# Eight buffers for W2's tiles, and one weight set loaded in one run

## The chip, the core and the metric

The kernel runs on one core of one Trainium2 chip. The core has a matrix engine (TensorE, PE in the profile; its weight loads are PEld), a vector engine (DVE), a scalar engine (ACT), GpSimd (POOL) and a sync engine (SP), each with its own stream of instructions, which wait for each other by semaphores. Sixteen DMA engines move data between the chip's main memory, SBUF and other places in SBUF; in this kernel transfers are issued by SP and by ACT, each in the order of its stream (SPq and ACTq in the profile). The metric is the device time of one execution in microseconds (us).

## What is computed

A transformer block with attention and a gated MLP side by side, on one sequence of 2048 tokens of width 576, in bfloat16:

```python
def _A_ref(x, wqkv, wo):
    B, S, D = x.shape
    H = 32; Dh = D // H; W = 256
    ...
    scores = jnp.einsum("bhqd,bhkd->bhqk", q, k) * (Dh ** -0.5)
    mask = (idx[:, None] - idx[None, :] >= 0) & (idx[:, None] - idx[None, :] < W)
    ...
    return (lambda x, *d: x.transpose(*d))(o, 0, 2, 1, 3).reshape(B, S, D) @ wo

def _B_ref(x, w1, w3, w2):
    gate = jnp.einsum("bsd,df->bsf", x, w1)
    up = jnp.einsum("bsd,df->bsf", x, w3)
    h = _silu(gate) * up
    out = jnp.einsum("bsf,fd->bsd", h, w2)
    return out

x = A_x
xn = _layernorm(x, axis=-1)
return x + _A_ref(xn, A_wqkv, A_wo) + _B_ref(xn, B_w1, B_w3, B_w2)
```

There are 32 heads of width 18, the attention looks back 256 tokens, and the MLP's inner width is 4608.

## The kernel before

The tokens are cut into four chunks of 512 (`NC` = 4, numbered 0 to 3). Every chunk goes through the same stages on TensorE:

- the q, k and v projections (`proj_part`, L437), whose results ACT and DVE put into `stage` and `va`; DMA copies (L502) move q and k from `stage` into the layout that the scores need (`qv`, `kv`), eight groups of four heads;
- 36 units (`unit_pairs`, L664): a unit makes 128 of the 4608 inner columns, gate and up, by nine pairs of matmuls of 64 rows, the two of a pair side by side. Five pairs read the normalized input from `xnT`, four from `xnS`, a copy with the two halves of the partitions exchanged (L402). ACT (L673) and DVE (L679, L682) make the unit's column of `hT` of it. Between the units stand the score matmuls (L557), eight groups in turn, with their exponentials on ACT (L566) and masks on POOL (L593), and the products with v (`pv`, L614);
- the W2 stage (`p2_list`, `p2_item`): two halves of 288 output columns, each with nine tiles of W2 (`fc` = 0 to 8), so 18 tiles a chunk. A tile is 512 x 288 numbers (288 KB) in an SBUF buffer of 128 x 4 x 288 and is read by 16 matmuls (L715). At a half's last tile, the attention's output is multiplied with `wo` into the same banks (L721, reading `oT`), DVE adds x (L728) and SP stores the result (L730). The last pair of head groups' `pv` stands after the 20th item of the W2 stage, and the six copies that bring its result into `oT` follow on SP (`o_pack`, L651).

**Gate/up weights.** A chunk needs nine weight sets of W1 and W3, each for four units. A set is loaded by six transfers of 192 KB on SP (`load_part`, L323). They rotate over three buffers, `w13_0` to `w13_2`; the fourth set of chunk 0 goes into columns 18 to 26 of `hT`, which are still empty then. `owed` counts transfers that are allowed; `owe_part` issues one after the fourth and one after the last pair of a unit, each waiting for the matmul named. The last set of each chunk lies in `w13_1`, and the next set for that buffer, the next chunk's third, is asked for during the next chunk's projections. So `w13_1` holds nothing of use during the W2 stage.

**W2's tiles.** There are four buffers, `w2_0` to `w2_3`. A running count over all chunks picks the buffer. The first four loads are issued by SP in units 20 to 26 of chunk 0. Each later one is issued on ACT when the last matmul of a tile is written down, so it waits for that tile's matmuls and goes into its buffer: tile i's end asks for tile i + 4, and the last four tiles of a chunk ask for the first four of the next.

**The rows of x.** `load_x` (L299) loads 128 rows. Chunk 1's first two are asked for in the projections of chunk 0, after the key copies that `span_last(0, 2)` issues; the other two in units 8 and 17. Their first use is the layer norm's statistics (L358) from unit 20 on.

What orders DMA on an engine is the order in which the program writes the instructions: a transfer that waits for a semaphore holds up all that stand behind it on the same engine.

Of the kernel before, what the change touches and what calls it, by code (L numbers as in the profile page):

```python
# [164 lines left out]
def bass_parallel_sum__sliding_block__glu_gated_swiglu__prompt_kernel(  # L165
# [18 lines left out]
    NC = S // CH  # L184
# [13 lines left out]
    with ExitStack() as es:  # L198
# [96 lines left out]
        def load_x(t, eng="sp"):  # L295
            nonlocal xp_ctr
            s = xp_ctr % NXP
            xp_ctr += 1
            add(eng, lambda e: e.dma_start(xp[s][:], x2[t * 128:(t + 1) * 128, :]), w=[("xp", s)], dma=f"xp{s}")  # L299
            return s  # L300
# [37 lines left out]
                owed -= 1  # L338
                load_part((op,))

        n2fill = 0

        def load_w2(eng="sp"):
            nonlocal n2fill
            if n2fill >= NC * 2 * NFC:
                return
            s = n2fill % NW2
            half, fc = divmod(n2fill % (2 * NFC), NFC)
            n2fill += 1
            add(eng, lambda e: e.dma_start(  # L350
                w2[s][:], B_w2[fc * 512:(fc + 1) * 512, half * HD:(half + 1) * HD].rearrange("(fl p) d -> p fl d", p=128)),
                w=[("w2", s)], dma=f"w2_{s}")


        def ln_stats(t, s, part):
# [331 lines left out]
        def p2_list(c):  # L687

            seq = []
            for half in range(2):  # L690
                base = c * 2 * NFC + half * NFC
                for fc in range(NFC):
                    sl = (base + fc) % NW2
                    edge = fc == NFC - 1 or (half == 1 and fc == 0)
                    pairs = [(fl, tt) for fl in range(4) for tt in range(TB)]
                    if edge:
                        pairs = [(fl, tt) for tt in range(TB) for fl in range(4)]
                    for n, (fl, tt) in enumerate(pairs):
                        seq.append(("w2", half, fc, fl, tt, sl, n == len(pairs) - 1))
                        if fc == NFC - 1 and fl == 3:  # L700
                            seq += [("wo", half, fc, kd, tt, sl, False) for kd in range(5)]
                            seq.append(("out", half, fc, 0, tt, sl, False))
            return seq
# [3 lines left out]
        def p2_item(c, item, xs):  # L707
            nonlocal of_ctr
            what, half, fc, k, tt, sl, last = item
            d0 = half * HD  # L710
            bank = PS[:, ACC[tt], 0:HD]
            key = [("ps", ACC[tt])]
            if what == "w2":
                f = fc * 4 + k
                add("pe", lambda e: e.matmul(  # L715
                    bank, hT[:, f, tt * 128:(tt + 1) * 128], w2[sl][:, k, :], start=(f == 0), stop=False),
                    r=[("h", f), ("w2", sl)], **{"w" if f == 0 else "j": key})
                if last:
                    load_w2("act")
            elif what == "wo":  # L720
                add("pe", lambda e: e.matmul(  # L721
                    bank, oT[:, k, tt * 128:(tt + 1) * 128], wo[:, k, d0:d0 + HD], start=False, stop=(k == 4)),
                    r=[("oT", j) for j in range(G // 2)] + ["oTz", "wo", "woz"], j=key)
            else:
                o = of_ctr % NOF
                of_ctr += 1
                t = c * TB + tt
                add("dve", lambda e: e.tensor_tensor(ofin[:, o, :], bank, xp[xs[tt]][:, d0:d0 + HD], ALU.add),  # L728
                    r=key + [("xp", xs[tt])], w=[("of", o)])
                add("sp", lambda e: e.dma_start(out2[t * 128:(t + 1) * 128, d0:d0 + HD], ofin[:, o, :]),  # L730
                    r=[("of", o)], dma=f"out{o}")
# [93 lines left out]
        for what in [("q", 0), ("q", 1), ("q", 2), ("q", 3), ("8", 7), None]:  # L825
            got = proj_begin(0, what) if what else proj_end()
            if got == ("q", 0):
                load_w13((), 4)
                span_main(0, 2, "act")
                load_w13((), 2)  # L830
            elif got == ("q", 2):
                span_last(0, 2)
                for t in (TB, TB + 1):
                    xslot[t] = load_x(t)

        PV_COST, PV_AFTER = 6.6, 20
        main, rest = span_main, span_last
# [5 lines left out]
        for c in range(NC):  # L843
# [3 lines left out]
            plan = near if c + 1 < NC else {}  # L847
            stat, apply, xt = ({v[k]: i for i, v in plan.items()} for k in range(3))
            loads = {8: (2,), 17: (3,)} if c + 1 < NC else {}
            total = 9 * NF + len(att) + 3 * PV_COST  # L850
            if c:
                total += 9 * sum(COST[kind] for kind, _ in PROJ)
# [59 lines left out]
            for u in range(NF):  # L912
                at_u = u
                if c == 0 and u == 0:
                    owed += 12
                if u in loads:
                    for i in loads[u]:
                        xslot[(c + 1) * TB + i] = load_x((c + 1) * TB + i)
                b0 = jobs[u] = job()
                for n in range(9):  # L920
                    into = nxt - (clock + 9 - n)
                    if done < len(att) and (clock >= nxt or (n == 8 and into < 3 and clock >= soon)):
                        spaced_step()
                    op = unit_pairs(c, u, n, n + 1, b0[0])
                    clock += 1
                    if n in (3, 8):
                        owe_part(op)
                unit_tanh(u, b0[0])
                if u % 4 == 3 and u < NF - 4 and (c or u != 15):
                    owed += 6  # L930
                if next_pv in pv_ready and clock >= pv_ready[next_pv] and next_pv < 3:
                    j = next_pv
                    next_pv += 1
                    banks = job()
                    pv(c, j, banks)
                    clock += PV_COST
                    for g in (2 * j, 2 * j + 1):
                        for s in range(NS):
                            if pt_of[(c, g, s)][0] != "h":
                                free.append(pt_of[(c, g, s)])  # L940
                    later(u, lambda b=banks: (pv_out(b[0], 0), pv_out(b[1], 1), o_scale(0)))
                    later(u + 1, lambda j=j: (o_turn(2 * j, 0), o_turn(2 * j, 1), o_scale(1)))
                    later(u + 2, lambda j=j: o_turn(2 * j + 1, 0))
                    later(u + 3, lambda j=j: (o_turn(2 * j + 1, 1), o_pack(j, "sp")))
                unit_h(u, b0[0])
                for what in side.pop(u, []):
                    what()
                if u in stat:
                    t = (c + 1) * TB + stat[u]
                    for part in range(2):  # L950
                        ln_stats(t, xslot[t], part)
                if u in xt:
                    xn_send((c + 1) * TB + xt[u])
                if u in apply:
                    t = (c + 1) * TB + apply[u]
                    ln_apply(t, xslot[t])
                for span, a, b, n0, n1, eng in late_spans.get(u, []) if c == 0 else []:
                    span(a, b, only=slice(n0, n1), **({"q_eng": eng} if span is main else {"eng": eng}))
                if c == 0 and u in (8, 9, 10, 11):
                    buf, key = ((wo, "woz"), (oT, "oTz"))[(u - 8) // 2]  # L960
                    part = buf[64:128, 4, :] if u % 2 else buf[96:128, 0:4, :]
                    add("dve", lambda e, part=part: e.memset(part.bitcast(dt.float32), 0.0), **{"j" if u % 2 else "w": [key]})
                if c == 0 and u == 13:
                    for t in range(4):
                        rows = A_wo[252 * (t // 2):252 * (t // 2) + 252, :].rearrange("(s p d) f -> p s d f", p=2, d=Dh)[t % 2, :, :, :]
                        add("sp", lambda e, t=t, rows=rows: e.dma_start(wo[0:126, t, :], rows),
                            r=["woz"], dma="wo", **{"j" if t else "w": ["wo"]})
                    add("sp", lambda e: e.dma_start(wo[0:72, 4, :], A_wo[504:576, :]), r=["woz"], j=["wo"], dma="wo")
                if c == 0 and u in (20, 22, 24, 26):
                    load_w2()  # L970
                if u == 29:
                    xs = [load_x(c * TB + tt) for tt in range(TB)]
            assert done == len(att) and next_pv == 3, (done, next_pv)
# [4 lines left out]
            if c + 1 < NC:  # L978
                for g in range(G):
                    keep_keys(g)  # L980
            banks = ()
            for n, item in enumerate(p2_list(c)):
                p2_item(c, item, xs)
# [54 lines left out]
```

## Time and profile before

| | us |
|---|---|
| median of 3 runs | 562.51 |
| lowest and highest of the 3 | 562.33, 562.85 |
| the profiled execution | 562.53 |
| its span in the profile | 560.8 |
| TensorE busy | 555.4 |
| DVE, ACT, POOL busy | 314.8, 253.1, 163.1 |

The granted TensorE clock was 1.00 in the profiled execution. By its matmul starts, the stages lie as follows: chunk 0's units begin at 21.98 us, and the W2 stages of chunks 0 to 3 begin at 102.12, 239.90, 377.90 and 516.29. The page of the profile holds, for the whole execution, the busy time of each engine, a row of digits for 40 equal slices (9 means 90% or more), the chain of work that ended last, and groups of instructions by line. The views of the trace show instructions in order of time (start, duration, engine, line, operation, tile, and in brackets the idle time before it with what ended it), the chain in order of time, and the busy time of each engine within chosen windows. In such windows the last three numbers are the granted clock, the DMA share, and GB/s. Every DMA adds to its semaphore as its parts land; "landing" is the last of these increments, which the trace holds with its time.

### The profile page before, as it was taken

The page shows a single profiled execution, that of the slowest core. Times are in us where ns is not written, and L with a number is a line of the kernel's source. Part 1 is how long each engine was busy: PE and PEld are TensorE (multiplying, and loading weights), DVE is VectorE, ACT ScalarE, POOL GpSimd, SP SyncE. Part 2 cuts the span into 40 slices and gives each one's busy share as a digit, 9 for nine tenths or more (in the row PEclk, how much of TensorE's full clock was granted, in tenths as well). Part 3 has the DMA queues.
Part 4 walks back from the last instruction along what each step waited for, and adds up shares of the span by engine and source line. Part 5 has one row for each costly group of instructions (what it writes and reads, how often), then busy time and mean ns, then how long its engine had stood idle before and what let it go on. Part 6 is the DMA issues. An engine that isn't in the chain of part 4 may idle for free.

```text
span 560.8 us, 15711 instructions
## 1 busy us (share of the span) xinstructions
PE 555.4 (99%) x6767; PEld 343.9 (61%) x6767; DVE 314.8 (56%) x587; ACT 253.1 (45%) x349; POOL 163.1 (29%) x383
## 2 busy tenths in 40 slices
PE   8999999999999999999999999999999999999998
PEld 4445455677665455477766645547777654555776
DVE  7468788710465778851046668883114567767211
ACT  4357776100287776600037776650004676675000
POOL 6313454400034445330003344532000333433000
PEclk9999999999999999999999999999999999999999
DMA  9988879886366467587626754868752675460552
GB/s 249 206 192 179 198 171 203 196 215 176 87 143 145 117 146 165 139 200 206 170 67 139 169 129 111 161 177 189 194 145 59 138 172 131 113 162 12 139 148 64
DMA packets 126685, 85.83 MB, mean 153 GB/s; under 512 B 34024, under 2 KB 124320, under 8 KB 126616
## 3 DMA queue, kind: packets, MB, share of 16 engines
q1 hardware_dynamic: 89076, 63.16, 49.5%
q10 hardware_dynamic: 37540, 21.66, 14.7%
q8 instruction: 53, 0.87, 0.7%
q14 instruction: 16, 0.13, 0.1%
HBM read 71.29 MB, written 2.36 MB: 131 GB/s over the span
## 4 chain that ended last, share of the span: by engine, by line
PE 97%; DMA 2%; DVE 1%; issue 0%; POOL 0%
PE ps L664 50%; PE ps L715 24%; PE ps L437 9%; PE ps L557 6%; PE ps L614 4%; PE ps L721 3%; DMA w<-in_B_w_dram 1%; DMA xp<-in_A_x_dram 0%; DVE xn L370 0%; DVE stats L358 0%; DVE stats L360 0%; DVE mv L361 0%; POOL rstd L364 0%; PE ps L382 0%; DVE ofin L728 0%
## 5 line engine op out<-in xcount | busy, mean ns | idle before, releaser
L664 PE MATMUL ps<-xnT,w 64*128 64x512 bf16 x1400 | 181.3, 376 | 0.1
L664 PE MATMUL ps<-xnS,w 64*128 64x512 bf16 x1120 | 153.9, 376 | 0.0
L715 PE MATMUL ps<-w,hT 128*128 128x288 bf16 x1152 | 147.3, 286 | 0.2 <-DMA w<-in_B_w_dram 0.2
L566 ACT ACTIVATE pt<-ps 128x1024 bf16<-128x1024 f32 (+1 forms) x112 | 113.1, 1010 | 63.4 <-PE ps L557 63.1
L679 DVE SCALAR_TENSOR_TENSOR gs<-th,ps 128x512 bf16<-128x512 bf16 x144 | 97.8, 679 | 77.8 <-ACT th L673 76.7
L715 PEld LDWEIGHTS ps<-w,hT 128*128 128x128 bf16 x1152 | 111.9, 98 | 30.9 <-issue 1.7
L664 PEld LDWEIGHTS ps<-xnT,w 64*128 64x128 bf16 x1400 | 69.9, 94 | 58.6 <-issue 0.5
L593 POOL TENSOR_TENSOR pt<-pt,mk 128x128 int32<-128x128 int32 (+1 forms) x199 | 80.3, 425 | 79.5 <-ACT pt L566 79.5
L682 DVE SCALAR_TENSOR_TENSOR hT<-gs,ps 128x512 bf16<-128x512 bf16 x144 | 98.9, 687 | 5.0
L673 ACT ACTIVATE th<-ps 128x512 bf16<-128x512 f32 x144 | 85.4, 593 | 24.0 <-PE ps L664 23.7
L664 PEld LDWEIGHTS ps<-xnS,w 64*128 64x128 bf16 x1120 | 57.0, 94 | 52.5
L728 DVE TENSOR_TENSOR ofin<-ps,xp 128x288 bf16<-128x288 f32 x32 | 14.6, 457 | 120.2 <-PE ps L721 120.2
L450 ACT ACTIVATE stage<-ps 128x512 bf16<-128x512 f32 x16 | 9.6, 597 | 146.1 <-PE ps L437 143.8
L593 POOL TENSOR_TENSOR hT<-hT,mk 128x128 int32<-128x128 int32 (+1 forms) x31 | 12.4, 421 | 170.7 <-ACT hT L566 170.7
L557 PE MATMUL ps<-qv,kv 64*128 64x320 bf16 (+4 forms) x528 | 52.5, 260 | 0.0
L557 PEld LDWEIGHTS ps<-qv,kv 64*128 64x128 bf16 x528 | 27.3, 94 | 25.8 <-issue 0.3
L437 PE MATMUL ps<-xnT,wp 64*128 64x512 bf16 (+1 forms) x360 | 38.7, 355 | 0.0
L566 ACT ACTIVATE stage<-ps 128x1024 bf16<-128x1024 f32 x24 | 24.6, 1023 | 12.6 <-PE ps L557 12.6
L636 DVE STREAM_TRANSPOSE od<-oq 128x256 bf16<-128x256 bf16 x64 | 25.8, 427 | 6.3 <-POOL oq L629 6.3
L437 PEld LDWEIGHTS ps<-xnT,wp 64*128 64x128 bf16 x360 | 19.0, 94 | 14.1 <-issue 0.7
L721 PE MATMUL ps<-wo,oT 128*128 128x288 bf16 x160 | 24.8, 286 | 0.0
L593 POOL TENSOR_TENSOR stage<-stage,mk 128x128 int32<-128x128 int32 (+1 forms) x42 | 17.0, 423 | 17.4 <-ACT stage L566 17.2
(59 smaller groups left out, 341.9 us busy)
## 6 DMA issues: line engine op xcount, KB each, us to landing
w<-in_B_w_dram SPq DMA_DIRECT2D x210, 192.0 KB, 4.1
w<-in_B_w_dram ACTq DMA_DIRECT2D x68, 288.0 KB, 3.1
xp<-in_A_x_dram SPq DMA_DIRECT2D x29, 144.0 KB, 4.3
out_dram<-ofin SPq DMA_DIRECT2D x32, 72.0 KB, 1.7
xnS<-xnT SPq DMA_DIRECT2D x8, 256.0 KB, 4.3
oT<-od SPq DMA_DIRECT2D x56, 36.0 KB
pt<-in_A_wqkv_dram SPq DMA_DIRECT2D x4, 288.0 KB, 6.5
hT<-in_B_w_dram SPq DMA_DIRECT2D x6, 192.0 KB, 5.1
```

What stands on the lines that cost most here:

```text
L437: op = add("pe", lambda e, out_=out_, st=st, mv=mv, n=n, r0=r0, first=first: e.matmul(out_, st, mv, start=first, stop=(part == 1 and n == ...
L557: add("pe", lambda e, r0=r0, out_=out_, kb=kb, q0=q0, nb=nb: e.matmul(out_, kb4[r0:r0 + 64, g, kb + NV - NB, :] if kb < 0 else kv[r0:r0 + ...
L566: add("act", lambda e: e.activation(pt_slot(sl)[:, 0:w, :], PS[:, SC[0]:SC[1] + 1, 0:w].rearrange("p r q -> p q r"), ACT.Exp, scale=scale) ...
L593: add("pool", lambda e, vb=vb, mm=mm: e.tensor_tensor(vb, vb, mm, ALU.mult), r=(key if n == 0 else []) + ["mk"], **{"w" if n == 0 else "j" ...
L614: add("pe", lambda e, p=p, q=q, pr=pr, sl=sl, g=g, pos=pos, q0=q0, nb=nb, col=col, first=first, n=n: e.matmul(PS[32 * q:32 * q + VW, banks ...
L636: add("dve", lambda e: e.transpose(od[i][:, g % 2, c0:c0 + CH // 2], oq[:, c0:c0 + CH // 2]), r=["oq", "oq0"], **{"j" if half or g % 2 els ...
L664: op = add("pe", lambda e, n=n, r0=r0, r=r, k=k, src=src: e.matmul(PS[:, b0 + r, :], wt[r0:r0 + 64, k, fl * 128:(fl + 1) * 128], src, star ...
L673: add("act", lambda e: e.activation(th[i][:], PS[:, bg, :], ACT.Tanh, scale=0.5), r=[("ps", bg)], w=[("th", i)])
L679: add("dve", lambda e: e.scalar_tensor_tensor(out=gs[i][:], in0=th[i][:], scalar=1.0, in1=PS[:, bg, :], op0=ALU.add, op1=ALU.mult), r=[("t ...
L682: add("dve", lambda e: e.scalar_tensor_tensor(out=hT[:, u, :], in0=gs[i][:], scalar=0.5, in1=PS[:, bu, :], op0=ALU.mult, op1=ALU.mult), r= ...
L715: add("pe", lambda e: e.matmul(bank, hT[:, f, tt * 128:(tt + 1) * 128], w2[sl][:, k, :], start=(f == 0), stop=False), r=[("h", f), ("w2", ...
L721: add("pe", lambda e: e.matmul(bank, oT[:, k, tt * 128:(tt + 1) * 128], wo[:, k, d0:d0 + HD], start=False, stop=(k == 4)), r=[("oT", j) fo ...
```

## The change

W2's tiles rotate over eight buffers in place of four. The four new ones are views of `w13_1` (`w2x`). `w2_at` picks the buffer: of each eight tiles of a chunk the first four go into `w2`, with a start that moves by two from chunk to chunk, the next four into `w2x`. At the start of each W2 stage, behind the last matmul of unit 35, ACT issues the loads of tiles 4 to 7 at once; then the end of tile i asks for tile i + 8 (i below 10), the ends of tiles 10 and 11 for the next chunk's tiles 0 and 1, and those of 16 and 17 for its tiles 2 and 3. Tiles 12 to 15 ask for nothing. SP still issues chunk 0's first four in units 20 to 26.

In chunk 0, the third weight set's six transfers are issued in one run after `span_last(0, 2)`, with no wait for matmuls, and `owed` starts with 6 instead of 12. The four x loads of chunk 1 move to units 11, 13, 15 and 17; in the other chunks they stay.

```diff
+        w2x = w13[1][:, :, :].rearrange("p a b -> p (a b)")[:, 0:NW2 * 4 * HD].rearrange("p (n k d) -> p n k d", n=NW2, d=HD)
+
+        def w2_at(c, i):
+            n = i % (2 * NW2)
+            if n < NW2:
+                s = (n + 2 * c) % NW2
+                return s, w2[s]
+            return n, w2x[:, n - NW2, :, :]
+
+        def load_w2(c, i, eng="act", after=()):
+            if c >= NC:
+                return
+            s, dst = w2_at(c, i)
+            half, fc = divmod(i, NFC)
             add(eng, lambda e: e.dma_start(
...
+                w=[("w2", s)], after=after, dma=f"w2_{s}")
+
+        def next_w2(c, i):
+            if i < 10:
+                load_w2(c, i + 8)
+            elif i < 12:
+                load_w2(c + 1, i - 10)
+            elif i >= 16:
+                load_w2(c + 1, i - 14)
...
-                base = c * 2 * NFC + half * NFC
                 for fc in range(NFC):
-                    sl = (base + fc) % NW2
+                    sl = half * NFC + fc
...
+                buf, wt = w2_at(c, sl)
                 add("pe", lambda e: e.matmul(
-                    bank, hT[:, f, tt * 128:(tt + 1) * 128], w2[sl][:, k, :], start=(f == 0), stop=False),
-                    r=[("h", f), ("w2", sl)], **{"w" if f == 0 else "j": key})
+                    bank, hT[:, f, tt * 128:(tt + 1) * 128], wt[:, k, :], start=(f == 0), stop=False),
+                    r=[("h", f), ("w2", buf)], **{"w" if f == 0 else "j": key})
                 if last:
-                    load_w2("act")
+                    next_w2(c, sl)
...
             elif got == ("q", 2):
                 span_last(0, 2)
-                for t in (TB, TB + 1):
-                    xslot[t] = load_x(t)
+                load_w13()
...
             loads = {8: (2,), 17: (3,)} if c + 1 < NC else {}
+            if c == 0:
+                loads = {11: (0,), 13: (1,), 15: (2,), 17: (3,)}
...
                 if c == 0 and u == 0:
-                    owed += 12
+                    owed += 6
...
                 if c == 0 and u in (20, 22, 24, 26):
-                    load_w2()
+                    load_w2(0, (u - 20) // 2, "sp")
...
+            for i in range(NW2, 2 * NW2):
+                load_w2(c, i, after=(last_pe(),))
```

More of the change, by code (lines that the diff above doesn't have):

```diff
@@ L339, in owe_part @@
                 load_part((op,))
[L341 to L345, printed above, removed]
+        w2x = w13[1][:, :, :].rearrange("p a b -> p (a b)")[:, 0:NW2 * 4 * HD].rearrange("p (n k d) -> p n k d", n=NW2, d=HD)
[7 more added lines that the diff above has]
+            if c >= NC:
                 return
-            s = n2fill % NW2
-            half, fc = divmod(n2fill % (2 * NFC), NFC)
-            n2fill += 1
+            s, dst = w2_at(c, i)
+            half, fc = divmod(i, NFC)
             add(eng, lambda e: e.dma_start(
-                w2[s][:], B_w2[fc * 512:(fc + 1) * 512, half * HD:(half + 1) * HD].rearrange("(fl p) d -> p fl d", p=128)),
-                w=[("w2", s)], dma=f"w2_{s}")
+                dst[:, :, :], B_w2[fc * 512:(fc + 1) * 512, half * HD:(half + 1) * HD].rearrange("(fl p) d -> p fl d", p=128)),
+                w=[("w2", s)], after=after, dma=f"w2_{s}")
[6 more added lines that the diff above has]
+                load_w2(c + 1, i - 14)
         def ln_stats(t, s, part):
```

## The prediction

> **What bounds the kernel now.** I read the page's shares first, then the chain of waits, then TensorE's timeline for gaps between matmul starts, then the windows for how full the DMA engines are.
>
> ```profile
> PE 555.4 (99%) x6767; PEld 343.9 (61%) x6767; DVE 314.8 (56%) x587; ACT 253.1 (45%) x349; POOL 163.1 (29%) x383
> DMA  9988879886366467587626754868752675460552
> PE 97%; DMA 2%; DVE 1%; issue 0%; POOL 0%
> L715 PE MATMUL ps<-w,hT 128*128 128x288 bf16 x1152 | 147.3, 286 | 0.2 <-DMA w<-in_B_w_dram 0.2
> w<-in_B_w_dram ACTq DMA_DIRECT2D x68, 288.0 KB, 3.1
> ```
>
> TensorE is busy 555.4 of 560.8 us and holds 97% of the chain, so only its gaps and its pace can be won. The pace is even: by the starts in the trace, the W2 matmuls (L715) follow each other every 122 or 123 ns, and the gate/up matmuls (L664), which start in pairs, every 215 to 217 ns a pair. Outside the first 10 us (warm-up and layer norm, untouched) three starts break it. One is in the gate/up loop:
>
> ```profile
> 35.58 1.24 PE L664 MATMUL ps<-xnT,w 64*128 64x512 bf16 x10
> 37.75 1.49 PE L664 MATMUL ps<-xnT,w 64*128 64x512 bf16 x10
> ```
>
> Ten matmuls that take 1.24 us take 1.49 here: a pair interval is 454 ns instead of 216, so 0.24 us. It is where unit 8 begins, the first reader of the third weight set. The set's last two parts are issued at 32.50 and 33.98 and take 4.1 us to land, so the last is there at 38.1; the reader was due at 37.97.
>
> The second is in chunk 2's W2 stage, and the chain shows it as time of a DMA:
>
> ```profile
> 399.57 1.97 PE ps L715 x16
> 401.56 6.05 DMA w<-in_B_w_dram
> 407.65 4.46 PE ps L715 x35
> ```
>
> A W2 tile asked for at 401.56, as its buffer came free, took 6.05 us beside the two 256 KB xnS copies of 400.5 and 401.1; with four buffers the cover was 5.9 us. The interval is 534 ns instead of 122: 0.41 us. A third, at 114.86, is 179 ns: 0.06 us. All three are waits for DMA, together 0.71 us of 560.8.
>
> **The change, part by part.** (1) Third weight set of chunk 0 in one run. Its six transfers no longer wait for matmuls of units 0 to 2 but stand in SP's queue where two x loads stood at 25.14. At 0.65 us an issue (3.00 us for 4 in the SP timeline, at most 0.75) they are out by 29.1 to 29.6 and, at the 4.1 to 5.2 us that these parts took to land, there by 34.8, 3 us ahead of 37.97. Gain 0.24 us, all on the path. Bounds: 0 if they were again late, 0.24 if not.
>
> What stands behind them moves too. The set in hT's columns follows at once (its waits are for units 0 to 2, over by 27.8), then three key copies of groups 2 to 4, formerly at 29.93, now at about 29.1 + 4 x 0.65 = 31.7. Even with the longest landing of that stretch (7.7 us) and two more issues, they are there by 41; the first score matmul of group 2 is the ninth score step, at 50.41. Nine us of cover, cost 0. The four x loads move to units 11, 13, 15, 17; their first reader is a statistic at 69.81, while unit 17 is at about 60: cost 0. The later sets of the chunk leave SP's queue earlier by up to two units, and are needed no earlier.
>
> (2) Eight W2 buffers. The count of loads (72 of 288 KB) and of matmuls is as before, and a matmul reading w13_1 instead of w2 has the same 128x288 form: 0. A tile is asked for eight tiles ahead, not four: cover grows from 5.9 to 13.7 us, against a slowest landing of some 6 us. Gain 0.41 + 0.06 = 0.47 us.
>
> (3) Four more loads at the start of each W2 stage, on ACT behind the last tanh.
>
> ```profile
> 102.23 0.60 ACT L673 ACTIVATE th<-ps 128x512 bf16<-128x512 f32 x1 [1.35 <-PE ps L664]
> 104.29 39.20 ACTq L350 DMA_DIRECT2D w<-in_B_w_dram  x18
> 146.80 0.60 ACT L450 ACTIVATE stage<-ps 128x512 bf16<-128x512 f32 x1 [43.97 <-PE ps L437]
> ```
>
> Four issues of 0.374 us fill 102.8 to 104.3, the gap before the load that tile 0's end releases at 104.29; ACT computes nothing until 146.80. ACT's cost is 0; without that gap, the next load would be at most 1.5 us later, with 13.7 us of cover. No later wait on ACT is added: the loads of tiles 12 to 15's turns are simply absent.
>
> But the transfers themselves come early, into a stretch where the DMA engines are full:
>
> ```profile
> 102.00:106.00 4.00, 4.00 (x97) 2.98 (x96) 3.41 (x7) 0.60 (x1) 3.51 (x10) 1.00 0.67 184
> 106.00:114.00 8.00, 8.00 (x67) 6.38 (x66) 2.93 (x8) 0.00 (x0) 1.35 (x2) 1.00 1.12 228
> 114.00:118.00 4.00, 4.00 (x35) 3.05 (x33) 0.00 (x0) 0.00 (x0) 0.00 (x0) 1.00 0.77 193
> 130.00:140.00 10.00, 10.00 (x84) 8.00 (x82) 0.00 (x0) 0.00 (x0) 0.00 (x0) 1.00 0.57 157
> 248.00:256.00 8.00, 8.00 (x67) 6.39 (x66) 0.56 (x2) 0.00 (x0) 0.00 (x0) 1.00 0.66 172
> 384.00:392.00 8.00, 8.00 (x68) 6.40 (x66) 1.68 (x5) 0.00 (x0) 0.72 (x2) 1.00 0.67 172
> ```
>
> The column before the last is the DMA share. In 130 to 140 only W2 tiles move, one per 1.96 us: 0.57 x 1.96 = 1.1 us of all sixteen engines for a tile (0.98 by 408 to 417, share 0.50). Four tiles are 3.9 to 4.5, say 4.2 us of extra work, at 102.6, at 240.4 and at 378.4. Who is late next? The last six oT copies (L651), due at the first wo matmul:
>
> ```profile
> 110.53 4.55 SPq L651 DMA_DIRECT2D oT<-od  x6
> 257.49 0.78 PE L721 MATMUL ps<-wo,oT 128*128 128x288 bf16 x5
> ```
>
> By the increments on their semaphore the last lands at 116.88, 255.03 and 393.00; wo starts at 119.47, 257.49 and 395.48: cover 2.6, 2.5 and 2.5 us. Does SP's small copy wait for ACT's backlog? In the first stage a small copy on ACT's otherwise empty queue (L502, issued 17.20) landed at 23.20, 6.0 us, while SP had eight large transfers under way; alone, at 147.43, the like took 2.0. So I count with service in order of issue, the dear case. Room that eats the backlog before the last oT copy: chunk 0, 0.33 x 4 + 0.23 x 1.3 = 1.6 us; chunk 1, full until 248 (share 1.00 from 238), then 0.34 x 6 = 2.0; chunk 2, 0.33 x 7.4 = 2.4. Left over as delay: 2.6, 2.2, 1.8 us. That just fits the cover; cost 0, the value I take. Bounds: 0, and 4.5 - 2.5 = 2.0 us a chunk, 6.0 in all, if no room were found. In chunk 3 no next chunk's weights load (share 0.40 over 516 to 561), cost 0.
>
> The Trainium skill, page "DMA: Bandwidth & Descriptors", section "Queues, rings and completion order", says that each DMA engine takes turns between the queues a packet at a time. By it the oT copies would hardly be delayed and the cost is 0 with room to spare; the row at 17.20 speaks against so clean a sharing.
>
> **Sum.** The profiled execution took 562.53 us (span 560.8 and 1.7 around it), 0.02 above the median, 562.51. 562.53 - 0.24 - 0.47 = 561.82, so 561.8 us, 0.13% less. Below 0.2% (1.1 us) a measurement of this kernel can't well be told from no change.
>
> **Rivals.** (A) The oT copies come late: the burst of four W2 tiles takes the DMA engines ahead of them, and TensorE stands at the first wo matmul of chunks 0, 1 and 2. It decides once the delay passes 2.5 us. For it: the share is above 1.00 in 106 to 114, my leftover for chunk 0 equals the cover, and 17.20 shows small copies waiting behind large ones. Against it: the shares leave room in chunks 1 and 2, and xnT, xnS and outputs have 5 us and more. Middle of the bounds, 0.9 us each: 561.8 + 2.7 = 564.5; to 567.8 at the end of the bounds; within 0.2% of before if only chunk 0 pays.
>
> (B) Nothing is won: the waits are so small (0.24, 0.41) that DMA jitter makes new ones, or the third set is late again since it now shares the engines with the q and k copies. 562.4. Against it: 3 us and 8 us of new cover.
>
> (C) The earlier weight transfers starve the attention of chunk 0: keys of group 2 after 50.41. It needs 9 us of delay; the longest landing there is 7.7. A missed score step would cost about 2 us: 563.8.
>
> (D) Faster by over 0.2%: that needs 1.1 us, and the trace shows 0.71 of waits; only waits that this one execution didn't have could give it. 561.2.
>
> **How the numbers follow.** Forecast 0.52; B 0.13; A 0.25 (0.20 of it above 0.2%, 0.05 within); C 0.02; D 0.08. Faster 0.08, same 0.52 + 0.13 + 0.05 = 0.70, slower 0.22. The likeliest case's own range is 561.4 to 562.4. For 8 in 10 the range goes to 561.2 below and into A up to 564.2, leaving half of D and the dearer half of A outside.
>
> **What would show it.** Right: unit 8's ten matmuls take 1.24 us; no L715 start interval above 135 ns but at the pv matmuls; the DMA piece is gone from the chain of chunk 2; ACT issues four loads at once after the last tanh; DMA share near 1.0 longer after 102, 240 and 378, and wo matmuls still starting about 17.35 us (chunk 0) after the W2 stage. Wrong: a gap before L721 in chunks 0 to 2, with oT landing more than 2.5 us after its old place (A); a new gap in units 8 to 16 (B, C).

## The result, and the profile after

| | us |
|---|---|
| before, median of 17 runs | 562.59 (562.10 to 563.22) |
| changed, median of 17 runs | 564.45 (563.15 to 565.89) |
| ratio | 1.0032, 95% interval 1.0023 to 1.0040 |
| the changed kernel's profiled execution | 565.61, span 563.8 |

The changed kernel is slower by 1.86 us, 0.3%. Its profiled execution is one of the dearer ones, 1.16 us above its median. The changed file is 13 lines longer above the places that matter, so L664, L715, L721 and L651 of before are L677, L728, L734 and L664 here, and the W2 loads of L350 are L355. On the page:

```profile
PE 555.4 (98%) x6767; PEld 350.1 (62%) x6767; DVE 314.9 (56%) x587; ACT 253.1 (45%) x349; POOL 163.5 (29%) x383
DMA  9998769993366457599335655869922674561730
L728 PE MATMUL ps<-w,hT 128*128 128x288 bf16 x1152 | 147.1, 286 | 0.0
L734 PE MATMUL ps<-wo,oT 128*128 128x288 bf16 x160 | 24.8, 286 | 3.2 <-DMA oT<-od 2.4
w<-in_B_w_dram ACTq DMA_DIRECT2D x68, 288.0 KB, 5.2
```

TensorE does the same 555.4 us of work in a span 3.0 us longer. The W2 matmuls (L728) no longer wait at all. The wo matmuls (L734), which never waited before, have 3.2 us of idle time ahead of them, put down to the DMA that fills `oT`. A W2 tile takes 5.2 us to land at the median; before, it took 3.1. The chain in order of time, in chunk 1's W2 stage:

```profile
253.77 6.45 DMA oT<-od
260.22 0.14 issue
260.36 0.77 PE ps L734 x5
```

and TensorE's timeline there:

```profile
255.75 2.74 PE L728 MATMUL ps<-w,hT 128*128 128x288 bf16 x21
260.36 0.77 PE L734 MATMUL ps<-wo,oT 128*128 128x288 bf16 x5 [1.87 <-DMA oT<-od]
```

The last of the six copies takes 6.45 us, and wo starts only when it is there. By matmul starts, the interval ahead of wo is 1.08 us in chunk 0, 2.16 in chunk 1 and 0.80 in chunk 2, against 0.12 where nothing waits: 0.95 + 2.03 + 0.67 = 3.65 us lost. The third weight set's gap is gone:

```profile
35.70 1.29 PE L677 MATMUL ps<-xnT,w 64*128 64x512 bf16 x10
37.86 1.29 PE L677 MATMUL ps<-xnT,w 64*128 64x512 bf16 x10
```

Unit 8's ten matmuls take as long as unit 7's. The 3.65 us lost and the 0.71 us of old gaps won give 2.94 us, and the two spans differ by 3.0. ACT's timeline at the start of chunk 0's W2 stage, and SP's when the copies are issued in chunk 1:

```profile
102.12 0.60 ACT L686 ACTIVATE th<-ps 128x512 bf16<-128x512 f32 x1 [1.35 <-PE ps L677]
102.13 42.13 ACTq L355 DMA_DIRECT2D w<-in_B_w_dram  x18
```

```profile
249.42 5.04 SPq L664 DMA_DIRECT2D oT<-od  x6
254.51 1.23 SPq L408 DMA_TRANSPOSE xnT<-xn  x1
```

The burst begins with the last tanh, and the six copies' issues take 5.04 us where they took 4.56 before. In the windows (the column before the last is the DMA share, the last GB/s):

```profile
102.00:106.00 4.00, 4.00 (x98) 3.04 (x97) 3.43 (x7) 0.60 (x1) 3.42 (x10) 1.00 0.95 232
106.00:114.00 8.00, 8.00 (x67) 6.38 (x66) 2.81 (x8) 0.00 (x0) 1.35 (x2) 1.00 1.19 222
114.00:118.00 4.00, 4.00 (x35) 3.20 (x33) 0.00 (x0) 0.00 (x0) 0.00 (x0) 1.00 1.14 261
130.00:140.00 10.00, 10.00 (x84) 7.98 (x83) 0.00 (x0) 0.00 (x0) 0.00 (x0) 1.00 0.23 61
248.00:256.00 8.00, 8.00 (x68) 6.37 (x67) 0.77 (x2) 0.00 (x0) 0.59 (x1) 1.00 1.16 262
```

The DMA share is now 0.95 to 1.19 from 102 to 118, it is 1.16 in 248 to 256, where it was 0.66, and 0.23 from 130 to 140, where it was 0.57: the work came forward. In 106 to 114 the share rose from 1.12 to 1.19, but the rate did not, 222 GB/s against 228. For this mix of transfers the engines were already at their limit, as I read it, and the burst found no place in these 8 us.

### The profile page after: what moved, and what is told of

It is laid out like the page before. It is cut to its first block, busy times and chain, and to the rows that moved or that the text cites. A ratio compares the mean times of both kernels' runs of the same rounds, so it can differ in the third digit from the quotient of the medians.

```text
span 563.8 us, 15711 instructions
## 1 busy us (share of the span) xinstructions
PE 555.4 (98%) x6767; PEld 350.1 (62%) x6767; DVE 314.9 (56%) x587; ACT 253.1 (45%) x349; POOL 163.5 (29%) x383
## 4 chain that ended last, share of the span: by engine, by line
PE 92%; DMA 3%; DVE 2%; SPq 1%; issue 1%; POOL 1%
PE ps L677 50%; PE ps L728 20%; PE ps L450 9%; PE ps L570 6%; PE ps L734 4%; PE ps L627 4%; DMA oT<-od 2%; SPq L664 1%; DMA xp<-in_A_x_dram 1%; POOL oq L642 0%; DVE od L649 0%; DVE xn L383 0%; DVE uq L636 0%; DVE stats L371 0%; DVE stats L373 0%
## 5 line engine op out<-in xcount | busy, mean ns | idle before, releaser
L677 PE MATMUL ps<-xnT,w 64*128 64x512 bf16 x1400 | 181.7, 376 | 0.0
L677 PE MATMUL ps<-xnS,w 64*128 64x512 bf16 x1120 | 154.6, 376 | 0.0
L728 PE MATMUL ps<-w,hT 128*128 128x288 bf16 x1152 | 147.1, 286 | 0.0
L728 PEld LDWEIGHTS ps<-w,hT 128*128 128x128 bf16 x1152 | 112.1, 98 | 30.3 <-issue 1.7
L677 PEld LDWEIGHTS ps<-xnT,w 64*128 64x128 bf16 x1400 | 72.6, 94 | 55.7
L677 PEld LDWEIGHTS ps<-xnS,w 64*128 64x128 bf16 x1120 | 59.1, 94 | 50.6
L734 PE MATMUL ps<-wo,oT 128*128 128x288 bf16 x160 | 24.8, 286 | 3.2 <-DMA oT<-od 2.4
```

Source lines behind the costliest of these rows:

```text
L677: op = add("pe", lambda e, n=n, r0=r0, r=r, k=k, src=src: e.matmul(PS[:, b0 + r, :], wt[r0:r0 + 64, k, fl * 128:(fl + 1) * 128], src, star ...
L728: add("pe", lambda e: e.matmul(bank, hT[:, f, tt * 128:(tt + 1) * 128], wt[:, k, :], start=(f == 0), stop=False), r=[("h", f), ("w2", buf) ...
L734: add("pe", lambda e: e.matmul(bank, oT[:, k, tt * 128:(tt + 1) * 128], wo[:, k, d0:d0 + HD], start=False, stop=(k == 4)), r=[("oT", j) fo ...
```

## The experiments

**1. The first chunk's part alone** (`e1_third_set`), on the kernel before:

```diff
             elif got == ("q", 2):
                 span_last(0, 2)
-                for t in (TB, TB + 1):
-                    xslot[t] = load_x(t)
+                load_w13()
...
+            if c == 0:
+                loads = {11: (0,), 13: (1,), 15: (2,), 17: (3,)}
...
-                    owed += 12
+                    owed += 6
```

> The kernel before with the first chunk's third weight set in one run (and its x loads moved), W2 as before. Theory 1 (the burst of four W2 tiles makes the last oT copies late): this part has no share in the loss; the 0.24 us gap at unit 8 is gone, the gap of 0.4 us at a W2 tile of chunk 2 stays, no gap ahead of the wo matmuls; 562.59 - 0.24 = 562.35 us, ratio 0.9996, no more than 0.06% from it. Theory 2 (the earlier weight transfers of chunk 0 cost the time): at least half of the loss is here, 563.5 us or more, ratio 1.0016 or more, with new gaps in units 8 to 20.

Measured: 562.23 us against 562.81, ratio 0.9987 (0.9979 to 0.9996). Unit 8 has no gap:

```profile
35.66 1.24 PE L664 MATMUL ps<-xnT,w 64*128 64x512 bf16 x10
37.83 1.24 PE L664 MATMUL ps<-xnT,w 64*128 64x512 bf16 x10
```

W2's waits for its tiles are still there in the profile: the matmul starts at 131.27 and 387.46 come 0.30 and 0.32 us late, at other tiles than in the kernel before. This part has no share in the loss. Between the medians it wins 0.58 us; the 0.24 expected lies at the edge of the interval.

**2. The W2 part alone** (`e2_eight_buffers`), the changed kernel with the first chunk put back:

```diff
             elif got == ("q", 2):
                 span_last(0, 2)
-                load_w13()
+                for t in (TB, TB + 1):
+                    xslot[t] = load_x(t)
...
-            if c == 0:
-                loads = {11: (0,), 13: (1,), 15: (2,), 17: (3,)}
...
-                    owed += 6
+                    owed += 12
```

> The changed kernel with the first chunk's third weight set and x loads put back as before; eight buffers and the burst of four loads stay. Theory 1 (burst, late oT copies): the whole loss is here, 564.45 + 0.24 = 564.7 us, ratio 1.0037 (1.002 to 1.005), gaps of 0.7 to 2.0 us ahead of the first wo matmul of chunks 0, 1 and 2. Theory 2 (chunk 0's earlier weights): 562.59 - 0.47 = 562.1 us, ratio 0.9992, no such gaps.

Measured: 565.38 us against 562.81, ratio 1.0050 (1.0033 to 1.0068). The whole loss is here. The gaps ahead of wo are 1.73, 0.12 and 0.52 us in its profile, so those of chunks 1 and 2 were smaller than expected. The third weight set was late by more than in the first profile:

```profile
37.88 0.38 PE L677 MATMUL ps<-xnT,w 64*128 64x512 bf16 x2
39.19 1.04 PE L677 MATMUL ps<-xnT,w 64*128 64x512 bf16 x8 [0.93 <-issue]
```

The pair interval is 1307 ns here, 1.09 us above 216, where the kernel before had shown 0.24. The same code's wait thus differs by 0.85 us between two executions, which may be why experiment 1 won more than 0.24 between the medians.

**3. Eight buffers without the burst** (`e3_no_burst`): until the first half's wo matmuls are passed, each tile's end asks for one tile, four ahead; then two at a time.

```diff
         def next_w2(c, i):
-            if i < 10:
-                load_w2(c, i + 8)
-            elif i < 12:
+            if i < 8:
+                load_w2(c, i + 4, after=(last_pe(),))
+            elif i < 11:
+                load_w2(c, 2 * i - 4, after=(last_pe(),))
+                load_w2(c, 2 * i - 3, after=(last_pe(),))
+            if i in (10, 11):
                 load_w2(c + 1, i - 10)
...
-            for i in range(NW2, 2 * NW2):
-                load_w2(c, i, after=(last_pe(),))
```

> The changed kernel with the four extra loads spread out: the ends of tiles 0 to 7 ask for the tile four ahead, and only the ends of tiles 8, 9 and 10, which lie behind the wo matmuls of the first half, ask for two each, so that the second half is eight ahead. Buffers, their places, number of loads and the first chunk as changed. Theory 1 (burst): no gap ahead of wo, the last oT copies take 2 to 3.6 us to land as in the kernel before, all three old gaps gone; 562.59 - 0.71 = 561.9 us, ratio 0.9987 (0.998 to 0.9995). Theory 3 (the buffers' place in the gate/up buffer, or their semaphores, cost the time): 564 us or more, ratio 1.0025 or more.

Measured: 561.97 us against 562.81, ratio 0.9981 (0.9972 to 0.9989). The last oT copy lands 2.2, 3.1 and 2.7 us after its issue in chunks 0 to 2, no gap stands ahead of wo, and the largest left at a W2 tile is 0.04 us. TensorE at chunk 1's first wo matmul (L737 in this file), and the windows of chunk 0:

```profile
255.82 1.63 PE L731 MATMUL ps<-w,hT 128*128 128x288 bf16 x12
257.29 0.78 PE L737 MATMUL ps<-wo,oT 128*128 128x288 bf16 x5
```

```profile
106.00:114.00 8.00, 8.00 (x67) 6.40 (x66) 2.77 (x8) 0.00 (x0) 1.35 (x2) 1.00 1.07 218
114.00:118.00 4.00, 4.00 (x35) 3.19 (x34) 0.00 (x0) 0.00 (x0) 0.00 (x0) 1.00 0.77 181
```

No idle time ahead of wo, and the share falls to 0.77 by 114, as in the kernel before; with the burst it stayed at 1.14. The buffers, their place and their semaphores cost nothing.

**4. The burst stays, the other load goes** (`e4_weights_later`): the next chunk's second weight set is loaded at the start of the W2 stage's second half.

```diff
-                if u % 4 == 3 and u < NF - 4 and (c or u != 15):
+                if u % 4 == 3 and u < NF - 8 and (c or u != 15):
                     owed += 6
...
+                elif n == 175:
+                    for _ in range(6):
+                        load_part((last_pe(),))
                 elif n == 300 and c + 1 < NC:
```

> The changed kernel with its burst, but the six transfers of the next chunk's second weight set, which run beside the burst at each W2 stage's start, are issued at the start of the W2 stage's second half instead. Theory 1 in the form that the DMA engines as a whole are full (about 5 us of weight transfers and 4.4 us of burst at once): taking 5 us out makes more room than the burst takes, no gap ahead of wo, last oT copy 2 to 4 us to land; 561.9 us, ratio 0.9987 (0.998 to 0.9997). Theory 1 in the form that any four W2 tiles issued ahead hold up SP's copies, whatever else runs: gaps stay, 563.5 us or more, ratio 1.0015 or more.

Measured: 561.90 us against 562.81, ratio 0.9984 (0.9975 to 0.9992). The windows, and TensorE at the same wo matmul as above:

```profile
106.00:114.00 8.00, 8.00 (x67) 6.40 (x66) 2.71 (x8) 0.00 (x0) 1.35 (x2) 1.00 0.88 239
114.00:118.00 4.00, 4.00 (x35) 3.19 (x34) 0.00 (x0) 0.00 (x0) 0.00 (x0) 1.00 0.88 204
248.00:256.00 8.00, 8.00 (x68) 6.38 (x66) 0.27 (x1) 0.00 (x0) 0.00 (x0) 1.00 0.72 174
```

```profile
255.73 1.63 PE L728 MATMUL ps<-w,hT 128*128 128x288 bf16 x12
257.20 0.78 PE L734 MATMUL ps<-wo,oT 128*128 128x288 bf16 x5
```

With the same burst at the same place, the share stays below 1 and wo starts with no idle time. So it is not the burst by itself but burst and weights together. They are of one size, 4 x 288 and 6 x 192 KB; experiment 3 spreads the one out, experiment 4 moves the other out of this stretch, and either is enough. Whether weights count for more than as many bytes of anything else, these two do not tell. Both versions beat the kernel before, and so the changed one.

**5. Half the burst** (`e5_burst_two`):

```diff
         def next_w2(c, i):
-            if i < 10:
-                load_w2(c, i + 8)
-            elif i < 12:
-                load_w2(c + 1, i - 10)
+            if i < 12:
+                load_w2(c, i + 6, after=(last_pe(),))
+            elif i < 14:
+                load_w2(c + 1, i - 12)
             elif i >= 16:
                 load_w2(c + 1, i - 14)
...
-            for i in range(NW2, 2 * NW2):
+            for i in (4, 5):
                 load_w2(c, i, after=(last_pe(),))
```

> The changed kernel with a burst of two W2 tiles instead of four at each W2 stage's start; the end of tile i asks for tile i + 6. Backlog theory: half the extra transfers (about 2 x 1.4 = 2.8 us of all DMA engines at the loaded rate) less the 1.6 to 2.4 us of room leaves 0.4 to 1.2 us of delay; the last oT copies take 3 to 4.5 us to land, within the cover, no gap ahead of wo; 561.9 to 562.2 us, ratio 0.998 to 0.9995. If any burst ahead of the copies costs its whole cover (a wait that doesn't scale with the backlog): gaps stay near 1 us a chunk, 564 us or more.

Measured: 562.24 us against 562.71, ratio 1.0000 (0.9989 to 1.0011), outside the range expected. The windows of chunk 0:

```profile
106.00:114.00 8.00, 8.00 (x68) 6.37 (x67) 2.80 (x8) 0.00 (x0) 1.35 (x2) 1.00 1.17 222
114.00:118.00 4.00, 4.00 (x35) 3.21 (x33) 0.00 (x0) 0.00 (x0) 0.00 (x0) 1.00 1.14 276
```

The engines are as full as with four tiles up to 118, only not as far behind. In its profiled execution (561.96 us) the mechanism is as expected: the last oT copies take 4.2, 3.9 and 3.2 us, there is no gap ahead of wo, and what is left of the cover is 0.8, 0.9 and 2.0 us. But the 12 runs go from 561.63 to 563.70, while experiments 3 and 4 stay within 561.71 to 562.23. With less than 1 us left, some executions may well miss it; no slower run of this version was profiled, so that stays open.

**6 and 7. Whose queue holds up the copies?** In chunk 3, SP's queue is empty in the W2 stage. On top of experiment 4, six spare loads of W2's size go into key space that is no longer used, in chunk 3 alone, ahead of the oT copies: on ACT (`e6_spare_act`) or on SP (`e7_spare_sp`). The loads are additional work; nothing reads them.

```diff
                     pv(c, 3, banks)
+                    if c == NC - 1:
+                        spare = kv[:, :, :, :].rearrange("p g b f -> p (g b f)")
+                        for k in range(6):
+                            add("act", lambda e, k=k: e.dma_start(
+                                spare[:, k * 4 * HD:(k + 1) * 4 * HD].rearrange("p (f d) -> p f d", d=HD),
+                                B_w2[k * 512:(k + 1) * 512, 0:HD].rearrange("(fl p) d -> p fl d", p=128)),
+                                after=(last_pe(),), dma=f"spare{k}", **{"j" if k else "w": [("k", g) for g in range(G)]})
```

> On top of the version with the later weights, and in chunk 3 alone, where SP's queue is empty: six spare W2-sized loads into key space no longer used, issued by ACT right behind the last pv matmul, so ahead of the six oT copies on SP. Order-of-issue theory (a copy waits behind everything issued earlier, on whichever queue): the first oT copy takes 4.5 us or more to land instead of 2.1, and wo of chunk 3 starts late by 1 us or more. Turn-taking theory (each DMA engine takes turns between SP's and ACT's queues): the oT copies take at most 3.5 us as before (2.1 to 3.3), wo of chunk 3 is on time.

> The same six spare loads at the same point of chunk 3, but issued by SP, ahead of the oT copies on their own queue. Both theories: the oT copies land late, the first 4.5 us or more after its issue. Order of issue: as late as with the loads on ACT, within 1 us. Turn-taking: later than there by 2 us or more.

Each of the two ran once; only its trace is used. In chunk 3 of these traces each of the six copies adds ten times to the semaphore that they share: once 1.1 to 1.4 us after its issue, with or without a backlog, and nine times as its data land. Without the first kind, and with the copies taken to land in order of issue, the n-th is complete with increment 9n at the earliest; for the sixth this is exact. By that they took, in us:

```
chunk 3          1st  2nd  3rd  4th  5th  6th   wo late by
experiment 4     2.1  3.3  2.8  3.4  2.8  2.6   0
6, loads on ACT  4.8  4.8  5.1  5.1  5.3  5.5   0.81
7, loads on SP   6.6  6.5  6.2  5.9  5.7  5.7   1.51
```

TensorE at wo of chunk 3, with the loads on ACT:

```profile
530.73 3.10 PE L728 MATMUL ps<-w,hT 128*128 128x288 bf16 x24
534.49 0.77 PE L734 MATMUL ps<-wo,oT 128*128 128x288 bf16 x5 [0.65 <-DMA oT<-od]
```

and with them on SP:

```profile
534.52 0.77 PE L734 MATMUL ps<-wo,oT 128*128 128x288 bf16 x5 [1.34 <-DMA oT<-od]
```

Neither expectation is met whole. With nothing on SP's queue ahead of them, the copies still take 1.5 to 2.9 us longer because of ACT's loads. That rules out turn-taking as it was expected here (at most 3.5 us), though not every form of sharing between the queues. Order of issue comes closer, but wo was late by 0.81 us, not 1, and the first copy took 1.8 us longer with the loads on SP, which is not within 1 us. By these numbers no copy lands more than 1.2 us before the tile that ACT issued last ahead of it, and the tiles land 0.98 us apart: the first copy, issued at 524.77, was complete at 529.60 at the earliest, behind the tile that ACT had issued at 522.62 (529.43) and ahead of the one of 524.29 (530.43); the last, issued at 528.84, landed at 534.35, with the tile of 528.03 (534.36). With the loads on SP's own queue the wait is 1.8 us more for the first copy and 0.2 more for the last. The Trainium skill's rule of turns between queues ("DMA: Bandwidth & Descriptors", section "Queues, rings and completion order") is therefore no ground for counting such a delay at nothing; no run here shows the turns themselves, and a queue of their own spared the copies 1.8 us at most.

**8. More cover** (`e8_pv_early`): the changed kernel, with the last pv ten matmuls earlier.

```diff
-                elif n == 19:
+                elif n == 9:
                     banks = (ring(), ring())
```

> The changed kernel with the last pv of a chunk after 10 items of the W2 stage instead of 20, so that it and the oT copies come up to 1.2 us earlier; the burst stays. If the loss is the delay beyond the cover: the copies' issue moves ahead by 0.5 to 1.2 us, each gap ahead of wo shrinks by about as much, to 0 to 1.2 us; 562.0 to 563.0 us, ratio 0.9985 to 1.001. If the copies only wait for the burst to drain, whenever they are issued: gaps as in the changed kernel, 564 us or more, ratio 1.002 or more.

Measured: 562.51 us against 562.71, ratio 0.9994 (0.9986 to 1.0003). The last copy is issued 0.68, 1.66 and 3.46 us earlier by the trace, of which 0, 0.2 and 2.3 are gaps that did not arise before it. It still takes 6.2, 5.3 and 5.1 us, against 5.9, 6.5 and 5.6 in the changed kernel: the delay is there as before. The gaps ahead of wo are 0.71 us in chunk 0, where the copy took 0.4 us longer, and none in chunks 1 and 2:

```profile
119.92 0.77 PE L734 MATMUL ps<-wo,oT 128*128 128x288 bf16 x5 [0.55 <-issue]
```

So the loss is what the delay has beyond the cover.

## Why the prediction was wrong

The forecast was 561.8 us, 0.13% faster than before; 564.45 us were measured, 0.3% slower.

**The three old waits** were read rightly. All are gone in the changed kernel and in experiments 3 and 4. Put at 0.71 us, their removal measured 0.84 and 0.91 us between medians in experiments 3 and 4, whose intervals hold 0.71 too. If the term was a little small, the third weight set is the likely place: one execution does not show a wait at its mean (experiment 2: 1.09 us for the one of 0.24), and experiment 1 alone won 0.58.

**The earlier weights of chunk 0** cost nothing (experiment 1), as the sum has it. **The four issues on ACT** cost nothing either, though they began at 102.12, with the last tanh and not behind it, and took 0.43 to 0.76 us each in place of 0.374.

**The step that failed** is in part (3): "Left over as delay: 2.6, 2.2, 1.8 us. That just fits the cover; cost 0, the value I take." What was late next (the six oT copies), what it delays (the first wo matmul), the cover (2.6, 2.5, 2.5 us) and the three chunks were right; the delay was mis-sized. For the last copy:

```
               took before  took after  delay  cover  issued late  gap by these  gap measured
chunk 0           2.50         5.87      3.4    2.6       0            0.8           0.95
chunk 1           2.58         6.45      3.9    2.5       0.5          1.9           2.03
chunk 2           2.57         5.58      3.0    2.5       0            0.5           0.67
```

The 0.13 to 0.17 us between the last two columns is about the step from landing to matmul, the 0.14 of "issue" in the chain. The half microsecond of chunk 1 is SP's third copy, which took 1.18 us to issue; at that moment ACT was issuing a tile for 2.73.

The delay was put too small because I took a DMA share below 1.00 for room, and a tile for 1.1 us wherever it runs. The rate shows both better. These are the windows from the start of each W2 stage to 0.9 us after the place where the last copy was issued before, first of the kernel before, then of the changed one:

```profile
102.12:115.29 13.17, 13.17 (x172) 10.26 (x171) 6.22 (x14) 0.60 (x1) 4.74 (x11) 1.00 0.94 206
239.90:253.35 13.45, 13.45 (x197) 10.62 (x196) 6.03 (x14) 0.60 (x1) 4.63 (x11) 1.00 0.88 193
377.90:391.34 13.44, 13.44 (x197) 10.61 (x196) 6.03 (x14) 0.60 (x1) 4.62 (x11) 1.00 0.86 188
```

```profile
102.01:115.18 13.17, 13.17 (x173) 10.38 (x172) 6.24 (x14) 0.60 (x1) 4.76 (x12) 1.00 1.11 227
240.74:254.19 13.45, 13.45 (x197) 10.62 (x196) 6.04 (x14) 0.60 (x1) 4.65 (x11) 1.00 1.15 222
380.75:394.19 13.44, 13.44 (x197) 10.62 (x196) 6.05 (x14) 0.60 (x1) 4.65 (x11) 1.00 1.16 239
```

By the last column, 277, 390 and 685 thousand bytes more were moved in chunks 0, 1 and 2, of the 1180 thousand in the burst's four tiles. At the rates of the changed kernel four tiles are 5.2, 5.3 and 4.9 us of work, not 4.2, and the room was 1.2, 1.8 and 2.9 us, not 1.6, 2.0 and 2.4. So the work of the burst was the larger mistake. The 903, 790 and 495 thousand bytes left over take 3.5, 3.7 and 2.1 us at the rate from there to the last landing (261, 213 and 231 GB/s), against 3.4, 3.9 and 3.0 measured. This ledger is an estimate worked out afterwards from the two profiles. It covers chunks 0 and 1; 0.9 us of chunk 2's delay stays open. That burst and weights together make the backlog is shown by experiments 3 and 4.

**Rival A** is what happened: its place, its mechanism and the point from which it decides (2.5 us). Its middle, 0.9 us a chunk or 2.7 in all, compares with 3.65 us in the profiled execution, and with 1.86 + 0.87 = 2.7 us between the medians, if 0.87 us (the mean of 0.84 and 0.91) is what the waits' removal is worth. It was given 0.25, because the copies were counted as just in time in all three chunks at once: a cost of 0 that hung on covers used up to 0.0 us in chunk 0 and 0.3 in chunk 1 should have carried half the chance or more. **B, C and D** found no support: the old waits did go, no new gap stands in units 8 to 16 for a late key, and the versions without the delay win 0.84 and 0.91 us, less than the 1.1 that D needs.

## What to carry to other kernels

Loading further ahead removes a wait only if the transfers are not brought into a stretch where the DMA engines are at their rate already; look there for the small transfer with a due time, and compare its cover with the bytes brought forward divided by the rate of that stretch. A cost of nothing that uses up all of a cover is a coin toss, not a zero. The same eight buffers, with the third weight set's part, win 0.16 to 0.19% when either the prefetch waits until the due copies are through or the other bulk load moves to where the engines have time.

## What the runs showed of the hardware

- Six small SP copies, alone on their queue, took 4.8 to 5.5 us behind ACT's backlog and 2.1 to 3.4 without it (experiments 6 and 4): another queue's backlog is not invisible.
- With a backlog on the DMA engines, issuing takes longer as well: ACT's issue of a W2 tile went from 0.374 us to as much as 2.73 (chunk 1 of the changed kernel).
- The DMA share does not stop at 1.00, and the rate at a share above 1.1 depends on what is moved. From 106 to 114 (weights, transposes and tiles) it was 228 GB/s before, 222 in the changed kernel and 212 in experiment 2, at shares of 1.12 to 1.19; from 525.3 to 528.2 in experiment 6, with hardly anything but tiles of 288 KB landing every 0.98 us, it was 302 at 1.16.
- Times spread more where TensorE waits for DMA: the kernel before lay between 561.92 and 563.95 us beside experiments 1 to 4, while the versions without such waits (3 and 4) stayed within 0.42 and 0.52 us, and experiment 1, which takes away the third weight set's wait alone, within 0.63. That this one wait makes most of the spread is likely, but not traced.
